# An attention and gated-MLP block on one core: moving the block transposes, scratch stores, weight loads and weight splits of the second norm

## The chip, the cores and the metric

The kernel runs on one core of one Trainium2 chip. The metric is the device time of one execution in microseconds (us); the time of a kernel is the median of several runs. The core has the engines PE (TensorE, matmuls), DVE (VectorE), ACT (ScalarE), POOL (GpSimd) and SP (SyncE). Each works through its own instructions in program order. Nearly all DMAs here are issued by SP on one queue.

## What is computed

Two residual branches on x of 2048 rows and 448 columns: attention with 16 heads of 28, then a gated MLP with a spatial mix over the rows. Each branch takes a layer norm that is scaled and shifted by columns computed from a vector c.

```python
h = layernorm(x) * (1 + ca) + sa
x = x + ga * attention(h, wqkv, wo)
h = layernorm(x) * (1 + cb) + sb              # the second norm
z = gelu(h @ w_in)                            # 2048 x 1792
z1, z2 = z[:, :896], layernorm(z[:, 896:])
g = w_sp @ z2 + b_sp                          # mixes rows
x = x + gb * ((z1 * g) @ w_out)
```

All data are float32.

## The kernel before, in words

Matmuls are made on float32 values split into a high and a low part, with products high-high, high-low and low-high; `STEPS` lists the eleven matmuls that make one product over the 448 rows of the contraction (three full chunks of 128, and a fourth of 64 whose high and low parts share one tile). Splitting a tile is a copy to the high part and a subtraction for the low one.

The order of instructions is written out by hand: each engine executes what the Python code issues, in that order, and waits on semaphores for its inputs. Tiles come from pools with a fixed number of buffers; seven PSUM banks go round (`bank`).

The stages are: the modulation columns and the first norm, the query, key and value products, attention (most of the span), the output product, the second norm, the first half of the w_in product (`z1_unit`), the second half (`z2_gemm`), the spatial mix, and the product with w_out. The change touches the stretch from the last output products to the end of the first half of the w_in product.

The 2048 rows form four groups of 512, index 0 to 3.

- `wo_tile(t)` (L1115) makes the output product of 128 rows on PE; `wo_add` (L1044) adds it to x on DVE and stores the result x2 to scratch through SP (L1047).
- `h2_stats(g)` (L1049) and `h2_norm(g)` (L1062) make the statistics and the normalized rows of group g; the power for the reciprocal deviation runs on POOL.
- Group 0 is transposed on PE by `ln_transpose` through `h2_first` (L1179). For its four column chunks, in the order 0, 2, 1, 3, ACT scales and copies, DVE subtracts, and then a function given as `after` is called with the chunk: here `late_tile` (L1210), which issues the last four output products in between.
- Groups 1 to 3 take another way. `h2_turn(g)` (L1079) transposes 32 x 32 blocks on DVE (L1086, four instructions). `h2_put(g)` (L1088) stores the blocks to a scratch tensor in DRAM with four DMAs (L1090). `h2_load(g)` (L1097) reads them back as rows of the transposed matrix with five DMAs (L1102 and L1104); it needs all four stores. `h2_group(g, cs)` (L1183) scales and splits the named column chunks, on ACT (L1187, L1188) and DVE (a subtraction, shown as L151).
- `z1_unit(g, f)` (L1196) makes eleven matmuls (L1199) for column block f of seven and row group g, the gelu on ACT (L1203) and the store of z1 (L1204). The loop at L1250 runs over 28 units.
- Between the units, `H2_AT` (L1240) says behind which unit which step of the norm is issued. `win_load` (L1108) loads rows of the other half of w_in; `win_prep` (L1112) splits them. For w_out, `wout_load` (L1224), `wout_part` (L1228: a product on DVE at L1230, a copy on ACT, a subtraction on DVE) and `wout_store` (L1236) run behind alternate units.

In a unit before the change, the w_out steps come ahead of the steps of `H2_AT`.

Of the kernel before, what the change touches and what calls it, by code (L numbers as in the profile page):

```python
# [99 lines left out]
def tile_adaln_mha_gmlp(ctx, tc, x, wqkv, wo, w_in, w_spT, b_sp, w_out, cT, w_mod0, w_mod, out):  # L100
# [881 lines left out]
    for h in range(H):  # L982
        a = h * NT
# [48 lines left out]
    t3 = ph3.enter_context(tc.tile_pool(name="t3", bufs=2))  # L1032
# [29 lines left out]
    def h2_norm(g):  # L1062
        mv, rs, _ = mv3.pop(g)
        if g == 0:
            nb = t3.tile([128, 4], F32, name="nb3")
            dve.scalar_tensor_tensor(out=nb, in0=mv[:, :, 0], scalar=-1.0, in1=rs, op0=ALU.mult, op1=ALU.mult)
        for tt in range(4):
            xt = x3[4 * g + tt]
            if g == 0:
                act.activation(xt[:, :D], xt[:, :D], AF.Identity, scale=rs[:, tt : tt + 1], bias=nb[:, tt : tt + 1])  # L1070
                pool.tensor_copy(xt[:, D:], xt[:, 384:D])
            else:
                dve.tensor_scalar(
                    out=xt[:, :D], in0=xt[:, :D], scalar1=mv[:, tt, 0:1], scalar2=rs[:, tt : tt + 1], op0=ALU.subtract, op1=ALU.mult
                )
# [3 lines left out]
    def h2_turn(g):  # L1079
        if g == 1:  # L1080
            b = fh.tile([128, 4 * 896], F32, name="turn", tag="heapE")
        else:
            b = t3.tile([128, 4, 512], F32, name="turn", tag="x3", bufs=3).rearrange("p a b -> p (a b)")
        blocks[g] = b[:, 0:1792].rearrange("p (b t i) -> p b t i", t=4, i=32)
        for tt in range(4):
            dve.transpose(blocks[g][:, :, tt, :], x3.pop(4 * g + tt)[:, :D])  # L1086

    def h2_put(g):  # L1088
        for a in range(4):
            sp.dma_start(  # L1090
                hs_scr[g - 1].rearrange("(b j) n -> j b n", j=32)[:, :, a * 128 : (a + 1) * 128],
                blocks[g][32 * a : 32 * a + 32].rearrange("p b t i -> p b (t i)"),
            )
# [14 lines left out]
    def win_load(i, p):  # L1108
        raw_in[i] = raw = p.tile([128, 896], F32, name="raw_in", bufs=1)
        sp.dma_start(raw, w_in[i * 128 : (i + 1) * 128, FH : 2 * FH])  # L1110

    def win_prep(i, lo_eng):  # L1112
        weight_part(w2, i, raw_in.pop(i), act, lo_eng)

    def wo_tile(t):  # L1115
        wo_mm(t, STEPS)
        wo_add(t)
# [59 lines left out]
    t3b = ph3.enter_context(tc.tile_pool(name="t3b", bufs=2))  # L1177

    def h2_first(after):  # L1179
        xns = [x3.pop(t) for t in range(4)]  # L1180
        ln_transpose(xns, t3b, h2T[0], cols["cb"], cols["sb"], (act,) * 4, (dve,) * 4, None, after)
# [14 lines left out]
    def z1_unit(g, f):  # L1196
        ps_t = bank("z1_ps")
        for j, (a, b) in enumerate(STEPS):
            pe.matmul(ps_t, w1[:, b, f * 128 : (f + 1) * 128], h2T[g][:, a, :], start=j == 0, stop=j == NST - 1)  # L1199
        if not zbuf:  # L1200
            zbuf.append(t3.tile([128, 4, 512], F32, name="z1t", tag="x3", bufs=3))
        zt = zbuf[0][:, (7 * g + f) % 4, :]
        act.activation(zt, ps_t, AF.Gelu_apprx_tanh)  # L1203
        sp.dma_start(z1_scr[f * 128 : (f + 1) * 128, g * 512 : (g + 1) * 512], zt)  # L1204
# [3 lines left out]
        h2_stats(1, (t - 8,))  # L1208

    def late_tile(c):  # L1210
        if c == 3:
            h2_turn(1)
        wo_tile({0: 12, 2: 13, 1: 14, 3: 15}[c])
        if c == 0:
            h2_norm(1)

    h2_first(late_tile)
    h2_put(1)
    win_load(0, t3)
    win_load(1, t3b)  # L1220
    wo3 = ph3.enter_context(tc.tile_pool(name="wo3", bufs=2))
    wouts = {}

# [15 lines left out]

    H2_AT = {}  # L1240
    for g, at_g in (
        (1, ((1, h2_load), (3, h2_group, (0, 2)), (4, h2_group, (1,)), (5, h2_group, (3,)))),
        (2, ((0, h2_stats), (1, h2_norm), (2, h2_turn), (3, h2_put), (5, h2_load))),
        (2, ((8, h2_group, (0,)), (9, h2_group, (2,)), (10, h2_group, (1,)), (11, h2_group, (3,)))),
        (3, ((4, h2_stats), (5, h2_norm), (6, h2_turn), (7, h2_put), (9, h2_load))),
        (3, ((13, h2_group, (0,)), (14, h2_group, (2,)), (15, h2_group, (1,)), (16, h2_group, (3,)))),
    ):
        for n, fn, *a in at_g:
            H2_AT.setdefault(n, []).append((fn, g, *a))
    for g in range(NG):  # L1250
        for f in range(7):
            z1_unit(g, f)
            for fn, n in ((wout_load, 10), (wout_part, 11), (wout_store, 12)):
                if 0 <= 7 * g + f - n < 14 and (7 * g + f - n) % 2 == 0:
                    fn((7 * g + f - n) // 2)
            for fn, *a in H2_AT.get(7 * g + f, ()):
                fn(*a)
            if g == 1 and f in (3, 5):
                win_prep(f // 4, dve)
                win_load(2 + f // 4, (t3, t3b)[f // 4])  # L1260
            if g == 2 and f in (3, 5):
                win_prep(2 + f // 4, dve)
# [417 lines left out]
```

## Time and profile before

| | us |
|---|---|
| Time, median of 3 runs | 1385.21 |
| Lowest and highest of these runs | 1382.43, 1385.46 |
| The profiled execution, its own time | 1383.42 |
| Span of the profile, from first to last instruction | 1381.6 |
| DVE busy | 1113.8 |
| ACT busy | 805.1 |
| POOL busy | 361.3 |

The profile is one execution on the chip. All positions in time are microseconds from the first instruction of the span. A line of the timeline gives the start, the length, the engine, the line of the kernel, the operation with output and input tiles, and how many instructions are merged; in brackets stands the idle time of the engine just ahead and what ended it. SPq is SP issuing DMAs, which isn't counted as busy. The granted clock is the share of full TensorE clock that the chip allowed in a stretch. A busy share is an average over stages with different limits; what a change in one stage is worth is read in that stage.

### The profile page before, as it was taken

The page shows a single profiled execution, that of the slowest core. Times are in us where ns is not written, and L with a number is a line of the kernel's source. Part 1 is how long each engine was busy: PE and PEld are TensorE (multiplying, and loading weights), DVE is VectorE, ACT ScalarE, POOL GpSimd, SP SyncE. Part 2 cuts the span into 40 slices and gives each one's busy share as a digit, 9 for nine tenths or more (in the row PEclk, how much of TensorE's full clock was granted, in tenths as well). Part 3 has the DMA queues.
Part 4 walks back from the last instruction along what each step waited for, and adds up shares of the span by engine and source line. Part 5 has one row for each costly group of instructions (what it writes and reads, how often), then busy time and mean ns, then how long its engine had stood idle before and what let it go on. Part 6 is the DMA issues. An engine that isn't in the chain of part 4 may idle for free.

```text
span 1381.6 us, 20787 instructions
## 1 busy us (share of the span) xinstructions
PE 1368.9 (99%) x7050; PEld 973.5 (70%) x7050; DVE 1113.8 (81%) x1764; ACT 805.1 (58%) x1475; POOL 361.3 (26%) x371
## 2 busy tenths in 40 slices
PE   9999999999999999999999999989999999999998
PEld 8888665555555565556565655877898888888898
DVE  7898899999999999999999971753367777999752
ACT  6623676767666776667676769435325544555411
POOL 2134335253535264745640011200021000000000
PEclk9999999999999999999999999999999999999999
DMA  8465756677677667876673010677604665787553
GB/s 284 135 172 182 231 162 210 198 222 234 208 213 211 215 201 225 237 240 209 216 230 97 23 44 22 207 229 219 233 16 142 224 197 195 245 285 262 186 163 108
DMA packets 144279, 260.21 MB, mean 188 GB/s; under 512 B 22120, under 2 KB 42986, under 8 KB 141626
## 3 DMA queue, kind: packets, MB, share of 16 engines
q1 hardware_dynamic: 141454, 254.69, 59.0%
q10 hardware_dynamic: 2718, 4.19, 0.8%
q8 instruction: 55, 0.90, 0.3%
q14 instruction: 52, 0.43, 0.1%
HBM read 177.67 MB, written 76.34 MB: 184 GB/s over the span
## 4 chain that ended last, share of the span: by engine, by line
PE 94%; DMA 2%; DVE 1%; issue 1%; SPq 1%; ACT 0%; POOL 0%; ACTq 0%; DVEq 0%; POOLq 0%
PE st_ps L744 18%; PE mt L712 17%; PE o_ps L759 16%; PE z_ps L1429 5%; PE acc L1497 5%; PE acc L1496 5%; PE acc L1498 5%; PE pq L407 5%; PE z_ps L1199 3%; PE wo_ps L831 2%; PE pv L389 2%; PE y_ps L1568 2%; PE y_ps L1569 2%; PE y_ps L1567 2%; PE acc L1504 1%
## 5 line engine op out<-in xcount | busy, mean ns | idle before, releaser
L717 DVE TENSOR_REDUCE pm<-mt 128x1 f32<-128x512 f32 x1024 | 627.8, 681 | 7.9 <-PE mt L712 7.7
L748 ACT ACTIVATE P<-st_ps 128x512 f32<-128x512 f32 x1024 | 512.6, 640 | 203.4 <-PE st_ps L744 200.9
L744 PE MATMUL st_ps<-qst,kst 128*128 128x512 f32 x1024 | 409.7, 410 | 0.0
L712 PE MATMUL mt<-kst,qst 128*128 128x512 f32 x1024 | 401.8, 392 | 0.0
L744 PEld LDWEIGHTS st_ps<-qst,kst 128*128 128x128 f32 x1024 | 191.3, 188 | 139.0 <-DVE pm L717 65.3
L759 PE MATMUL o_ps<-P,V 128*32 128x512 f32 x2048 | 240.0, 597 | 0.0
L712 PEld LDWEIGHTS mt<-kst,qst 128*128 128x128 f32 x1024 | 192.5, 188 | 34.7 <-ACT P L748 0.8
L869 POOL TENSOR_TENSOR ws_raw<-ws_raw 128x512 f32<-128x512 f32 x112 | 143.2, 1286 | 143.3 <-DMA ws_raw<-in_w_spT_dram 86.3
L1413 ACT ACTIVATE heapB<-raw_sp 128x512 fp32r<-128x512 f32 x156 | 96.7, 630 | 98.4 <-PE acc L1498 71.5
L759 PEld LDWEIGHTS o_ps<-P,V 128*32 128x32 f32 x2048 | 59.4, 109 | 126.8 <-issue 86.4
L1496 PE MATMUL acc<-heapB,heapA 128*128 128x512 f32 x312 | 121.4, 389 | 0.0
L1498 PE MATMUL acc<-heapB,heapA 128*128 128x512 f32 x312 | 121.4, 389 | 0.0
L765 DVE TENSOR_TENSOR osb<-osb,o_ps 128x512 f32<-128x512 f32 x82 | 56.4, 688 | 64.6 <-PE o_ps L759 63.1
L151 DVE TENSOR_TENSOR heapB<-raw_sp,heapB 128x512 fp32r<-128x512 f32 x112 | 74.6, 688 | 28.0 <-ACT heapB L1413 27.9
L1497 PE MATMUL acc<-heapB,heapA 128*128 128x512 f32 x222 | 86.5, 390 | 0.0
L1498 PEld LDWEIGHTS acc<-heapB,heapA 128*128 128x128 f32 x312 | 58.6, 188 | 12.2
L1496 PEld LDWEIGHTS acc<-heapB,heapA 128*128 128x128 f32 x312 | 58.6, 188 | 12.2
L407 PE MATMUL pq<-heapD,heapD 128*128 128x512 f32 x196 | 61.8, 390 | 0.0
L151 POOL TENSOR_TENSOR ws_raw<-ws_raw 128x512 fp32r<-128x512 f32 x44 | 56.7, 1288 | 3.5
L785 POOL TENSOR_TENSOR osb<-osb,rb 128x512 f32<-128x512 f32 x15 | 19.3, 1289 | 112.1 <-DVE pm L717 80.9
L1497 PEld LDWEIGHTS acc<-heapB,heapA 128*128 128x128 f32 x222 | 41.7, 188 | 8.8 <-DVE heapB L151 0.3
L171 POOL TENSOR_TENSOR rsz<-rsz,mhalf 128x1 f32<-128x1 f32 x16 | 14.2, 890 | 116.0 <-DVE rsz L170 116.0
(224 smaller groups left out, 1674.2 us busy)
## 6 DMA issues: line engine op xcount, KB each, us to landing
ws_raw<-in_w_spT_dram SPq DMA_DIRECT2D x136, 256.0 KB
ws_scr<-ws_raw SPq DMA_DIRECT2D x112, 256.0 KB
ws_raw<-ws_scr SPq DMA_DIRECT2D x88, 256.0 KB
raw_sp<-ws_scr SPq DMA_DIRECT2D x88, 256.0 KB
raw_sp<-in_w_spT_dram SPq DMA_DIRECT2D x68, 256.0 KB
wl_scr<-ws_raw SPq DMA_DIRECT2D x44, 256.0 KB
kst<-qk_scr SPq DMA_DIRECT2D x45, 224.0 KB
qst<-qk_scr SPq DMA_DIRECT2D x45, 224.0 KB
```

Of the source, the lines that this page charges most:

```text
L151: eng.tensor_tensor(out=dst, in0=a, in1=hi.bitcast(F32), op=ALU.subtract)
L407: pe.matmul(pq, wqk[:, b, m * 128 : (m + 1) * 128], hT[g][:, a, :], start=j == 0, stop=j == NST - 1)
L712: pe.matmul(mt, qst[h % 3][:, t * 128 : (t + 1) * 128], kst[h % 3][:, kb * 512 : (kb + 1) * 512], start=True, stop=True)
L717: dve.tensor_reduce(out=pms[h][:, t, kb : kb + 1], in_=mt, axis=AX.X, op=ALU.max)
L744: pe.matmul(st, kst[h % 3][:, kt * 128 : (kt + 1) * 128], qst[h % 3][:, qb * 512 : (qb + 1) * 512], start=True, stop=True)
L748: act.activation(p, st, AF.Exp, scale=SCALE)
L759: pe.matmul(o[32 * qb : 32 * qb + 32, :], V[:, u % NT, h, :], ptiles.pop((u, qb)), start=u == a, stop=u == e - 1)
L869: pool.tensor_tensor(out=a, in0=a, in1=b, op=ALU.add if W_SUMS[v][2] > 0 else ALU.subtract)
L1413: act.activation(hi, raw[0], AF.Copy)
L1496: pe.matmul(o, zh[:, c], hi, start=p < 2 and kt == 0, stop=False, skip_group_check=p > 1)
L1497: pe.matmul(o, zh[:, c], lo, start=False, stop=False, skip_group_check=p > 1)
L1498: pe.matmul(o, zl[:, c], hi, start=False, stop=kt == 3, skip_group_check=p > 1)
```

## The change

`late_tile` issues the four block transposes of group 1 and their four stores behind the output product of chunk 2, where before the transposes stood ahead of the output product of chunk 3 and the stores behind the whole of `h2_first`. The first two loads of w_in rows move from ahead of the loop to behind units 4 and 5. The loads of group 1's transposed rows move from behind unit 1 to behind unit 0. In every unit the steps of `H2_AT` now come ahead of the w_out steps, and the w_out splits and stores come one unit later than before (offsets 12 and 13 in place of 11 and 12).

```diff
     def late_tile(c):
-        if c == 3:
-            h2_turn(1)
         wo_tile({0: 12, 2: 13, 1: 14, 3: 15}[c])
         if c == 0:
             h2_norm(1)
+        elif c == 2:
+            h2_turn(1)
+            h2_put(1)
 
     h2_first(late_tile)
-    h2_put(1)
-    win_load(0, t3)
-    win_load(1, t3b)
...
     for g, at_g in (
-        (1, ((1, h2_load), (3, h2_group, (0, 2)), (4, h2_group, (1,)), (5, h2_group, (3,)))),
+        (1, ((0, h2_load), (3, h2_group, (0, 2)), (4, h2_group, (1,)), (5, h2_group, (3,)))),
...
     for g in range(NG):
         for f in range(7):
             z1_unit(g, f)
-            for fn, n in ((wout_load, 10), (wout_part, 11), (wout_store, 12)):
+            for fn, *a in H2_AT.get(7 * g + f, ()):
+                fn(*a)
+            if (g, f) in ((0, 4), (0, 5)):
+                win_load(f - 4, (t3, t3b)[f - 4])
+            for fn, n in ((wout_load, 10), (wout_part, 12), (wout_store, 13)):
                 if 0 <= 7 * g + f - n < 14 and (7 * g + f - n) % 2 == 0:
                     fn((7 * g + f - n) // 2)
-            for fn, *a in H2_AT.get(7 * g + f, ()):
-                fn(*a)
```

## The prediction, made before the changed kernel was run

> **What bounds the kernel now.** I read the page first, then the timeline of TensorE (PE) around the second norm.
>
> ```profile
> span 1381.6 us, 20787 instructions
> PE 1368.9 (99%) x7050; PEld 973.5 (70%) x7050; DVE 1113.8 (81%) x1764; ACT 805.1 (58%) x1475; POOL 361.3 (26%) x371
> ```
>
> PE is busy for 99% of the span, so the end moves only where PE waits or runs slowly. Nearly all of its waiting lies in the first-half GEMM loop (L1199): 28 units of 11 matmuls, seven units for each row group of 512. The timeline gives start, length, work, and in brackets the idle time ahead.
>
> ```profile
> 900.54 17.86 PE L1199 MATMUL z_ps<-heapB,heapA 128*128 128x512 f32 x78
> 919.00 1.42 PE L1199 MATMUL z_ps<-heapB,heapA 128*128 128x512 f32 x5 [0.60 <-ACT heapB L1188]
> 920.85 1.23 PE L1199 MATMUL z_ps<-heapB,heapA 128*128 128x512 f32 x3 [0.43 <-ACT heapB L1188]
> 924.89 18.46 PE L1199 MATMUL z_ps<-heapB,heapA 128*128 128x512 f32 x68 [2.82 <-DVE heapB L151]
> 943.19 2.20 PE L1199 MATMUL z_ps<-heap,heapA 128*128 128x512 f32 x9
> 948.21 34.59 PE L1199 MATMUL z_ps<-heap,heapA 128*128 128x512 f32 x145 [2.82 <-DVE heap L151]
> 982.64 0.77 PE L1429 MATMUL z_ps<-heapD,heapB 128*128 128x448 f32 x3
> ```
>
> The first burst is row group 0 and one matmul of the next (the text calls the four groups index 0 to 3, the fourth column chunk of a group chunk 3): 17.86/78 = 0.229 us a matmul, 2.52 a unit. At that pace 308 matmuls take 70.5 us; the loop takes 982.64 - 900.54 = 82.1. So **11.6 us** are lost. The idle entries are 0.60 + 0.43 + 2.82 at the start of index 1 and 2.82 in index 2: 6.67. Most of the rest is the clock. In these windows of L1199 the columns are stretch, length, PE busy, weight loads busy, granted clock, DMA share and GB/s.
>
> ```profile
> 900.50:918.40 17.90, 17.86 (x78) 14.48 (x78) 1.00 0.80 238
> 924.90:943.20 18.30, 18.30 (x69) 14.85 (x70) 0.84 0.78 233
> 948.20:982.60 34.40, 34.39 (x145) 28.20 (x145) 0.96 0.68 224
> ```
>
> A mean clock of 0.84 over 18.3 us costs 2.9, and 0.96 over 34.4 costs 1.4: 4.3 us in which PE ran at half speed just behind the idle stretches. 6.7 + 4.3 leaves 0.6 for refilling after four stops.
>
> **The first stall (index 1)** comes through ACT and DVE:
>
> ```profile
> 904.59 0.60 ACT L1203 ACTIVATE z1t<-z_ps 128x512 f32<-128x512 f32 x1
> 910.73 0.60 ACT L1203 ACTIVATE z1t<-z_ps 128x512 f32<-128x512 f32 x1 [1.90 <-PE z_ps L1199]
> 916.10 0.82 ACT L1187 ACTIVATE hfull<-heapB,col_sb,col_cb 128x512 f32<-128x512 f32 x1 [4.77 <-DMA heapB<-hs_scr]
> ```
>
> ```profile
> 920.83 0.69 DVE L151 TENSOR_TENSOR heapB<-hfull,heapB 128x512 fp32r<-128x512 f32 x1 [1.16 <-ACT heapB L1188]
> 921.44 2.20 DVE L1055 BATCH_NORM_STATS2 st<-xl 128x6 f32<-128x448 f32 x4
> 924.15 0.69 DVE L151 TENSOR_TENSOR heapB<-hfull,heapB 64x512 fp32r<-64x512 f32 x1
> ```
>
> ACT waits 4.77 us for the scratch load of the transposed rows, scales and splits the four column chunks from 916.10, and the last split part (chunk 3, behind the statistics of index 3) ends at 924.84: T + 8.74, if T is the first scaling. PE goes on at 924.89. The load was late because of SP, which issues every DMA here in order:
>
> ```profile
> 894.70 8.26 SPq L1047 DMA_DIRECT2D x_scr<-xl  x4
> 903.01 3.14 SPq L1090 DMA_DIRECT2D hs_scr<-turn  x4
> 906.20 2.12 SPq L1110 DMA_DIRECT2D raw_in<-in_w_in_dram  x2
> 909.44 2.35 SPq L1102 DMA_DIRECT2D heapB<-hs_scr  x3
> ```
>
> The stores of the blocks go out behind the last of four x2 stores; two w_in loads follow; the loads go out 6.43 us after the first block store, and the first one lands 6.66 later (909.44 to 916.10).
>
> **The second stall (index 2)** has another cause:
>
> ```profile
> 944.83 0.62 DVE L1230 TENSOR_TENSOR raw_out<-raw_out,bc_gb 128x448 f32<-128x448 f32 x1 [5.00 <-DMA raw_out<-in_w_out_dram]
> 947.47 0.69 DVE L151 TENSOR_TENSOR heap<-hfull,heap 64x512 fp32r<-64x512 f32 x1 [0.74 <-ACT heap L1188]
> ```
>
> In unit 11 DVE stands 5.00 us before the w_out rows of L1230, with the split of chunk 3 (and ACT's copies) queued behind. PE starts 0.05 us after that split ends.
>
> **The change part by part.** Instructions are neither added nor removed; positions move.
>
> *Transposes earlier.* DVE around them:
>
> ```profile
> 896.28 0.69 DVE L151 TENSOR_TENSOR heapB<-hfull,heapB 128x512 fp32r<-128x512 f32 x1
> ...
> 897.42 0.69 DVE L151 TENSOR_TENSOR heapB<-hfull,heapB 128x512 fp32r<-128x512 f32 x1
> 898.51 0.62 DVE L1046 TENSOR_TENSOR xl<-xl,wo_ps 128x448 f32<-128x448 f32 x1 [0.41 <-PE wo_ps L831]
> ...
> 899.88 2.22 DVE L1086 STREAM_TRANSPOSE turn<-x 128x448 f32<-128x448 f32 x4
> ```
>
> The four transposes (2.22) now start at 897.42, in the place of the split of chunk 1, and end at 899.65. Behind them come the split of chunk 1 (to 900.3), the addition of wo tile 14 (900.9), the split of chunk 3 (901.5) and the addition of tile 15 (902.1). PE begins the loop at 900.54 and reads chunk 1's low part at its ninth step (902.4) and chunk 3 at its tenth (902.6): 2.1 and 1.1 us of cover. Cost nothing; if DVE ran over 1.1 us later, each further microsecond is one of PE.
>
> *Stores directly behind, w_in later, load one unit earlier.* SP issues the block stores at 899.7 instead of 903.0, 3.3 earlier, into an idle queue (next to last number: DMA share; last: GB/s):
>
> ```profile
> 896.00:898.00 2.00, 2.00 (x12) 1.85 (x11) 2.00 (x4) 0.90 (x2) 0.00 (x0) 1.00 0.07 26
> 904.00:906.00 2.00, 2.00 (x11) 1.65 (x9) 1.17 (x7) 1.43 (x3) 0.65 (x1) 1.00 0.78 199
> 908.00:910.00 2.00, 2.00 (x10) 1.65 (x10) 2.00 (x5) 0.60 (x1) 0.00 (x0) 1.00 0.98 206
> 914.00:916.00 2.00, 2.00 (x11) 1.65 (x10) 0.00 (x0) 0.00 (x0) 0.00 (x0) 1.00 1.06 366
> ```
>
> With the 6.43 us of before they have landed at 906.1. By then SP has issued the x2 stores 14 and 15 (to 903.7) and the z1 store of unit 0, whose gelu ends at 905.19. So the loads go out at 906.1 instead of 909.44. Landing: at most 6.66 later as before, 912.8. But the queue ahead held two w_in loads (0.92 MB) and two z1 stores; now two x2 stores (0.46 MB) and one z1 store (0.26 MB fewer). 0.72 MB less at the 366 GB/s of the full queue is 2.0 us: **910.8**, which I take. ACT can't start chunk 0 before the gelu of unit 3 ends (911.33), so T = 911.3 and the last split ends at 920.1. PE wants it at the tenth step of unit 7: 900.54 + 7 x 2.52 + 9 x 0.229 = 920.2. The stall goes, with 0.1 to spare; T = 912.8 would leave 1.4. Below that, no gain is to be had: PE doesn't start the loop earlier.
>
> What 1.4 us of idle do to the clock no row shows: 0.60 and 0.43 left it at 1.00, 2.82 halved it, which cost 2.9 and 1.4. So 0 to 2.9 beside the 1.4, and 0 is nearer to the rows of under 1 us.
>
> ```profile
> 924.00:925.00 1.00, 0.11 (x1) 0.11 (x1) 0.81 (x2) 0.00 (x0) 0.73 (x1) 0.50 0.73 260
> ```
>
> The Trainium skill ("TensorE: Matmul & The Clock Gate", Part 1, "What's actually happening") says that the clock falls to half after at least one idle window of about 3.4 us and comes back after a busy one. By it neither 2.82 us here should have halved the clock, and 1.4 us would cost 1.4 alone; the trace shows 0.50 behind 2.82, so the row decides and I keep the upper end.
>
> *The same order for index 2 and 3: what is late next.* The block stores of index 2 follow the z1 store of unit 3 and go out at about 911.8:
>
> ```profile
> 915.28 3.43 SPq L1090 DMA_DIRECT2D hs_scr<-turn  x4
> ...
> 922.80 1.27 SPq L1102 DMA_DIRECT2D heap<-hs_scr  x3
> ```
>
> Store to load took 7.52 us; that gives loads at 919.3, landed at 926.0. The moved w_in loads lie in this stretch, one ahead of the loads and one behind. ACT takes the four chunks behind the gelus of units 8 to 11; the last gelu is ready at 900.54 + 12 x 2.52 = 930.8, so chunk 3 is split by 933.5. PE wants it at 937.9: 4.4 us to spare.
>
> *w_out splits one unit later, behind the steps of the norm.* The split of chunk 3 no longer waits for w_out; the second stall goes (2.82 + 1.4 + its refill). The wait itself remains: in unit 12, DVE's product waits for the w_out rows and ACT's copy for DVE; behind them stand the w_in split of unit 12, then gelu 13 and the chunks of index 3. The rows of index 3, and the first w_out load:
>
> ```profile
> 928.04 2.21 DVE L1086 STREAM_TRANSPOSE turn<-xl 128x448 f32<-128x448 f32 x4
> ```
>
> ```profile
> 940.45 0.38 SPq L1226 DMA_DIRECT2D raw_out<-in_w_out_dram  x1
> ```
>
> The transposes of index 3 ended 5.4 us behind the last split of index 1 (930.25 - 924.84), so now at 925.5; with the 7.52 of index 2 the loads go out at 933.0 and, 3 us of issuing later, the first w_out load at 936.0. From issue to use it took 4.4 (940.45 to 944.83): DVE goes on at 940.4, ACT behind its copy at 941.0. ACT then has one w_in copy (0.9), four gelus (0.60 each), four chunks (0.82 + 0.6 each) and one more w_out copy (0.6): 9.6 us, to 950.6, and DVE's split ends 0.7 later at 951.3. PE wants chunk 3 of index 3 at 955.5. Seven PSUM banks let PE run on meanwhile. Hidden, with 4.2 to spare.
>
> **Sum.** 11.6 lost, all of it removed, less 0.2 for the thin margin at index 1: 11.4. The profiled execution took 1383.42 (span 1381.6): 1372.0. The four times shown, 1382.43, 1383.42, 1385.21 and 1385.46, have a mean of 1384.1, 0.7 above it, so I predict **1372.7**.
>
> **Rivals.** *A, the forecast, 0.66:* 1371 to 1374.
> *B, the first stall shrinks but stays, 0.17:* the loads land as slowly as before, because the block stores and loads are limited by themselves. For it: 199 GB/s with 0.78 to 0.98 of the engines' time. Against: 0.72 MB less ahead. 1.4 to 4.3 us remain: 1374 to 1377.
> *C, for index 1 the change doesn't do what it says, 0.08:* the blocks leave earlier but a wait on SP (a store, or a load that waits for all four block stores) eats the 3.3 us. Then only the second stall goes, 2.82 + 1.4 + 0.2: about 1379.7. Against: SP has nothing to wait for between 903.7 and 905.2.
> *E, the w_out wait on ACT becomes the bound, 0.09:* as worked out, ACT may be freed up to 941.0 + 4.2 = 945.2 without harm; later than that, every microsecond is one of PE, plus up to 2.9 of slow clock. It ends slower than before if w_out lands past 945.2 + 11.4 - 2.9 = 953.7, 17.7 us after its issue at 936.0; a few microseconds earlier it is no difference. For it: SP, one queue, holds all. Against: 4.4 us in the trace. Slower 0.05, same 0.04.
>
> **How the numbers follow.** Range 1370.0 (the lowest run less 11.6, and 0.8 of scatter) to 1378.0 (B's end and a microsecond): A and B, 0.83. Faster by over 0.2% (2.8 us, about what a measurement of this kernel can tell from no change): A, B and C, 0.91; same 0.04; slower 0.05.
>
> **What would show it.** L1199 in one burst of 308 matmuls in 70 to 71 us at clock 1.00; L1090 issued first near 899.7 and L1102 near 906; ACT's L1187 of index 1 starting straight behind the gelu of unit 3; DVE's wait at L1230 still there, in unit 12, with PE busy beside it. An idle entry of over 1 us near 918 to 922 speaks for B; ACT behind L1230 with PE idle past 945 for E. I am wrong if the loads land after 912, or if the next stage gives back what this one gains.

## The result, and the profile after

| | before | after |
|---|---|---|
| median, us | 1384.19 (4 runs, 1382.43 to 1385.46) | 1370.17 (4 runs, 1369.99 to 1370.81) |
| profiled execution, us | 1383.42 | 1370.01 |
| span, us | 1381.6 | 1368.2 |

The changed kernel takes 0.990 of the time before, with a 95% interval of 0.9883 to 0.9918. The forecast was 1372.7 us, in a range of 1370.0 to 1378.0; the measured time is 2.5 us below the one and 0.2 us above the lower end of the other.

The busy line of the changed kernel's page:

```profile
PE 1361.4 (100%) x7050; PEld 968.0 (71%) x7050; DVE 1112.8 (81%) x1764; ACT 805.2 (59%) x1475; POOL 361.8 (26%) x371
```

The same instructions ran; PE's busy time fell by 7.5 us, 5.5 of it in the loop L1199, since a matmul at half clock counts as busy for longer (up to 0.79 us each in that loop before, at most 0.47 now). The timeline of PE through the loop L1199:

```profile
899.28 35.19 PE L1199 MATMUL z_ps<-heapB,heapA 128*128 128x512 f32 x154
934.31 35.07 PE L1199 MATMUL z_ps<-heap,heapA 128*128 128x512 f32 x154
969.22 0.77 PE L1429 MATMUL z_ps<-heapD,heapB 128*128 128x448 f32 x3
```

and its window (stretch, length, PE busy, weight loads busy, granted clock, DMA share, GB/s):

```profile
899.30:969.20 69.90, 69.90 (x308) 57.55 (x307) 1.00 0.87 274
```

No bracket with an idle time is left, and the clock is 1.00 throughout. The loop takes 969.22 - 899.28 = 69.9 us in place of 82.1. Its DMA share rose from 0.73 over the whole loop of before (227 GB/s) to 0.87 (274): nearly the same bytes, 18.6 and 19.2 MB, in less time.

The first row group that comes through scratch memory (index 1), on SP, ACT and DVE of the changed kernel:

```profile
898.41 3.01 SPq L1090 DMA_DIRECT2D hs_scr<-turn  x4
901.52 2.69 SPq L1047 DMA_DIRECT2D x_scr<-xl  x2
904.30 0.38 SPq L1204 DMA_DIRECT2D z_scr<-z1t  x1
905.31 1.27 SPq L1102 DMA_DIRECT2D heapB<-hs_scr  x3
```

```profile
909.47 0.60 ACT L1203 ACTIVATE z1t<-z_ps 128x512 f32<-128x512 f32 x1 [1.90 <-PE z_ps L1199]
909.97 0.80 ACT L1187 ACTIVATE hfull<-heapB,col_sb,col_cb 128x512 f32<-128x512 f32 x1
...
940.99 0.58 ACT L1230 ACTIVATE wout<-raw_out 128x448 fp32r<-128x448 f32 x1 [7.94 <-DVE raw_out L1228]
...
947.41 0.58 ACT L1230 ACTIVATE wout<-raw_out 128x448 fp32r<-128x448 f32 x1 [1.29 <-DVE raw_out L1228]
```

```profile
918.01 0.69 DVE L151 TENSOR_TENSOR heapB<-hfull,heapB 64x512 fp32r<-64x512 f32 x1
...
940.33 0.62 DVE L1228 TENSOR_TENSOR raw_out<-raw_out,bc_gb 128x448 f32<-128x448 f32 x1 [7.04 <-DMA raw_out<-in_w_out_dram]
...
951.72 0.69 DVE L151 TENSOR_TENSOR heap<-hfull,heap 64x512 fp32r<-64x512 f32 x1 [1.16 <-ACT heap L1188]
```

The loop began 1.26 us earlier than in the profile of before, so 1.26 us of every position here come from that. ACT goes straight from the gelu of unit 3 to the first scaling; the last split of index 1, behind DVE's statistics of index 3, ends at 918.70, and PE wants it at 899.28 + 7 x 2.497 + 9 x 0.227 = 918.80 (seven units of eleven matmuls at the pace of the burst, 0.227 us, and nine matmuls more). DVE still waits 7.04 us for w_out and ACT 7.94, now in unit 12 and with PE busy beside it, since PE's burst from 934.31 on has no idle entry.

### The profile page after: what moved, and what is told of

Same layout as the page of the kernel before. It is cut to its first block, busy times and chain, and to the rows that moved or that the text cites. A ratio compares the mean times of both kernels' runs of the same rounds, so it can differ in the third digit from the quotient of the medians.

```text
span 1368.2 us, 20793 instructions
## 1 busy us (share of the span) xinstructions
PE 1361.4 (100%) x7050; PEld 968.0 (71%) x7050; DVE 1112.8 (81%) x1764; ACT 805.2 (59%) x1475; POOL 361.8 (26%) x371
## 4 chain that ended last, share of the span: by engine, by line
PE 96%; issue 1%; DVE 1%; DMA 1%; POOL 0%; ACTq 0%; DVEq 0%; POOLq 0%; SPq 0%
PE st_ps L744 18%; PE mt L712 17%; PE o_ps L759 16%; PE z_ps L1429 5%; PE acc L1498 5%; PE acc L1497 5%; PE acc L1496 5%; PE z_ps L1199 5%; PE pq L407 5%; PE wo_ps L831 3%; PE pv L389 2%; PE y_ps L1569 2%; PE y_ps L1567 2%; PE y_ps L1568 2%; PE acc L1506 1%
## 5 line engine op out<-in xcount | busy, mean ns | idle before, releaser
L1432 ACT ACTIVATE z<-z_ps 128x448 f32<-128x448 f32 x32 | 17.4, 545 | 48.0 <-PE z_ps L1429 48.0
```

## The experiments

Theory: two stalls were removed. The first (index 1) was a matter of when the loads of the transposed rows land, the second (index 2) of chunk 3 standing behind the w_out wait on DVE and ACT; each also cost a stretch of half clock. The rivals were that the two are separate and simply add up, that w_out was hidden anyway, and that the w_out wait becomes the new bound. The diffs are against the changed kernel where nothing else is said. Each comparison has the kernel before on the same chip, 1383.5 to 1383.7 us.

**e1: the kernel before, a second profile.**

> The kernel before, once more, for a second profile of it. Theory: 1.26 us of the measured gain lie ahead of the loop, where the two kernels are the same, and come from a clock of 0.74 to 0.92 between 5 and 15 us that this execution of before happened to have; the loop L1199 takes 82.1 us again, give or take one half-clock window of about 1.5 us, so 1382 to 1386, and the slow clock at the start need not appear. Rival: before always starts with the slow clock, and the change removes it: 0.74 to 0.92 at 5 to 15 us again.

Measured: 1383.62 us, ratio 1.0002 [0.9993, 1.0011]. Two rows of the timeline of its loop, and the early windows of the first profile of before, with the granted clock as the third number from the end:

```profile
924.06 17.32 PE L1199 MATMUL z_ps<-heapB,heapA 128*128 128x512 f32 x68 [2.82 <-DVE heapB L151]
...
947.91 35.29 PE L1199 MATMUL z_ps<-heap,heapA 128*128 128x512 f32 x145 [4.50 <-DVE heap L151]
```

```profile
5.00:10.00 5.00, 4.88 (x37) 4.76 (x36) 4.05 (x12) 1.60 (x5) 1.61 (x2) 0.92 1.04 401
10.00:15.00 5.00, 4.68 (x25) 4.23 (x24) 3.75 (x12) 3.27 (x8) 0.00 (x0) 0.74 1.03 402
```

In e1 these two early windows are at 1.00. Of the thirteen profiles of this study three have the slow start (before, e4 and e6), two of them of kernels with the early stores; it belongs to an execution, not to a kernel. So the 1.26 us ahead of the loop, most of which that start accounts for, are no effect of the change. The loop of e1 took 983.04 - 899.47 = 83.6 us, 1.5 longer than in the first profile. PE ran only one half-clock window (3.41 us) behind the first stall, came to index 2 two microseconds sooner, and waited there 4.50 in place of 2.82: its restart, 947.91 against 948.21, was set by w_out, whose first rows DVE used at 944.53 against 944.83, and not by PE.

**e2: the part for index 1 alone.**

```diff
+            for fn, n in ((wout_load, 10), (wout_part, 11), (wout_store, 12)):
+                if 0 <= 7 * g + f - n < 14 and (7 * g + f - n) % 2 == 0:
+                    fn((7 * g + f - n) // 2)
             for fn, *a in H2_AT.get(7 * g + f, ()):
                 fn(*a)
             if (g, f) in ((0, 4), (0, 5)):
                 win_load(f - 4, (t3, t3b)[f - 4])
-            for fn, n in ((wout_load, 10), (wout_part, 12), (wout_store, 13)):
-                if 0 <= 7 * g + f - n < 14 and (7 * g + f - n) % 2 == 0:
-                    fn((7 * g + f - n) // 2)
```

> The changed kernel, with the w_out steps back in their old places (split in unit 11, ahead of the steps of the norm). Theory: the first stall is gone, so PE reaches row group index 2 some 9 us earlier, while the w_out rows land at about 940 as in the changed kernel; chunk 3 of index 2 is then split at 943.6 and PE wants it at 936.4: the second stall grows from 2.8 to about 7.3 us, and with 1.4 to 2.9 us of half clock behind it the time is 1378.9 to 1380.5. Rival (the two stalls are separate and keep their prices): the second stall is 2.8 us again and costs 4.5 with its clock: 1374 to 1376.

Measured: 1378.94 us, ratio 0.9971 [0.996, 0.9981]. Its PE and DVE:

```profile
943.19 34.68 PE L1199 MATMUL z_ps<-heap,heapA 128*128 128x512 f32 x145 [6.69 <-DVE heap L151]
```

```profile
939.81 0.62 DVE L1228 TENSOR_TENSOR raw_out<-raw_out,bc_gb 128x448 f32<-128x448 f32 x1 [7.71 <-DMA raw_out<-in_w_out_dram]
941.08 0.62 DVE L151 TENSOR_TENSOR wout<-raw_out,wout 128x448 fp32r<-128x448 f32 x1 [0.64 <-ACT wout L1230]
942.44 0.69 DVE L151 TENSOR_TENSOR heap<-hfull,heap 64x512 fp32r<-64x512 f32 x1 [0.74 <-ACT heap L1188]
```

The first stall is gone, and a good part of what that frees is given back: the second stall grows from 2.82 to 6.69 us. In index 2 PE is ready for its tenth step 8.9 us earlier than in the first profile of before (936.50 against 945.39), while DVE's first use of w_out moves by only 5.0 us (939.81 against 944.83).

**e3: the w_out part alone** (against the kernel before).

```diff
-            for fn, n in ((wout_load, 10), (wout_part, 11), (wout_store, 12)):
+            for fn, *a in H2_AT.get(7 * g + f, ()):
+                fn(*a)
+            for fn, n in ((wout_load, 10), (wout_part, 12), (wout_store, 13)):
                 if 0 <= 7 * g + f - n < 14 and (7 * g + f - n) % 2 == 0:
                     fn((7 * g + f - n) // 2)
-            for fn, *a in H2_AT.get(7 * g + f, ()):
-                fn(*a)
```

> The kernel before, with only the w_out splits and stores one unit later and behind the steps of the norm. Theory: the first stall stays (0.6, 0.4 and 2.8 us of idle, about 2.9 us of half clock), the second goes: 1377.5 to 1380. Rival (w_out is hidden anyway and the second stall only follows from the first, through late chunks of index 2): the second stall stays, 1383 to 1385.

Measured: 1377.66 us, ratio 0.9957 [0.9945, 0.997].

```profile
923.61 17.30 PE L1199 MATMUL z_ps<-heapB,heapA 128*128 128x512 f32 x68 [2.81 <-DVE heapB L151]
940.75 35.07 PE L1199 MATMUL z_ps<-heap,heapA 128*128 128x512 f32 x154
```

The first stall stays, index 2 and 3 run through. The two parts alone gain 4.7 (e2) and 6.0 (e3), the whole change 13.5 against the same runs of before (14.0 against its own): about 3 us more than their sum. Beside the first stall the second cost 6.0 us; with the first gone it costs 8.8 (13.5 less 4.7), because PE then arrives at it earlier by more than w_out does.

**e4: w_in loads ahead of the loop.**

```diff
     h2_first(late_tile)
+    win_load(0, t3)
+    win_load(1, t3b)
...
-            if (g, f) in ((0, 4), (0, 5)):
-                win_load(f - 4, (t3, t3b)[f - 4])
```

> The changed kernel, with the first two loads of w_in back ahead of the loop. Theory: SP spends 2.1 us on them ahead of the loads of the transposed rows, and 0.92 MB stand ahead in the queue; the first scaling of index 1 moves from 910.0 to 911.5 to 912.6, chunk 3 is late by the same 1.5 to 2.6 us, and half clock may add 0 to 2.9: 1371.5 to 1375.7. Rival (the early stores alone leave room enough): 1370.2, within 0.5.

Measured: 1374.88 us, ratio 0.9937 [0.9925, 0.995]. PE, SP and ACT:

```profile
922.47 17.35 PE L1199 MATMUL z_ps<-heapB,heapA 128*128 128x512 f32 x68 [2.36 <-DVE heapB L151]
```

```profile
906.74 1.89 SPq L1102 DMA_DIRECT2D heapB<-hs_scr  x3
```

```profile
913.66 0.81 ACT L1187 ACTIVATE hfull<-heapB,col_sb,col_cb 128x512 f32<-128x512 f32 x1 [2.44 <-DMA heapB<-hs_scr]
```

**e5: transposes and stores late.**

```diff
     def late_tile(c):
+        if c == 3:
+            h2_turn(1)
         wo_tile({0: 12, 2: 13, 1: 14, 3: 15}[c])
         if c == 0:
             h2_norm(1)
-        elif c == 2:
-            h2_turn(1)
-            h2_put(1)
 
     h2_first(late_tile)
+    h2_put(1)
```

> The changed kernel, with the block transposes and their stores back in their old places (w_in still later, loads still behind unit 0). Theory: SP issues the stores at about 901.9 in place of 898.4, the loads go out at 908.8 in place of 905.3, the first scaling of index 1 moves from 910.0 to 912.2 to 913.5: PE idles 2.2 to 3.5 us at the tenth step of unit 7 and runs one or two windows at half clock (1.7 or 2.9): 1374 to 1376.6. Rival (with the w_in loads out of the way the late stores are covered): 1370.2, within 0.5.

Measured: 1371.91 us, ratio 0.9914 [0.9899, 0.9929], less than expected.

```profile
920.14 15.71 PE L1199 MATMUL z_ps<-heapB,heapA 128*128 128x512 f32 x68 [1.45 <-DVE heapB L151]
```

```profile
908.60 1.29 SPq L1102 DMA_DIRECT2D heapB<-hs_scr  x3
```

```profile
911.34 0.82 ACT L1187 ACTIVATE hfull<-heapB,col_sb,col_cb 128x512 f32<-128x512 f32 x1 [1.53 <-DMA heapB<-hs_scr]
```

The two together separate the two edits for index 1. From the issue of the first load to its use take 913.66 - 906.74 = 6.92 us in e4, with the two w_in loads ahead of it, and 911.34 - 908.60 = 2.74 in e5, without. The two runs differ in other transfers too; the changed kernel differs from e4 by w_in alone. There the semaphore of this load was complete at 908.17, 2.86 us behind its issue at 905.31; in e4 it was at 913.58, 6.84 behind. So the 0.92 MB of w_in cost 4.0 us in the queue and, with e4's loop beginning 1.16 us later, 0.3 us on SP. They are the larger cause (e4 lost 4.7 us against the changed kernel, e5 1.7). The late stores cost 1.45 us of idle, and the clock stayed at 1.00 behind it (68 matmuls in 15.71 us, 0.231 each, against 0.255 in e4).

**e6: the loads of index 1 behind unit 1.**

```diff
-        (1, ((0, h2_load), (3, h2_group, (0, 2)), (4, h2_group, (1,)), (5, h2_group, (3,)))),
+        (1, ((1, h2_load), (3, h2_group, (0, 2)), (4, h2_group, (1,)), (5, h2_group, (3,)))),
```

> The changed kernel, with the loads of the transposed rows of index 1 back behind unit 1. Theory: the z1 store of unit 1 is ready at 905.1, and SP couldn't send the loads before 905.3 anyway, since the block stores had not landed: no difference, 1370.2 within 0.5. Rival (the unit's place on SP matters): the loads go out a unit, 2.5 us, later, and 2 to 4 us are lost: 1372 to 1375.

Measured: 1370.92 us, ratio 0.9905 [0.989, 0.9919]. The first half of the loop is one burst again:

```profile
900.60 35.19 PE L1199 MATMUL z_ps<-heapB,heapA 128*128 128x512 f32 x154
```

The time is 0.75 us above the changed kernel's, a little more than was expected, but the loop has no idle time, and this execution has the slow clock at 5 to 15 us, so its loop starts at 900.60. The first load was complete 10.36 us behind the start of the loop in place of 8.89 (910.96 and 908.17), and ACT began the first scaling at 10.68 and 10.69. So this edit of the change gains 1.5 us of spare time, and no time that the profiles show.

**e7 and e8: which half of the w_out edit matters.** e7 keeps the steps of the norm ahead and takes the w_out offsets back to 11 and 12; e8 keeps 12 and 13 and puts the w_out steps ahead again.

```diff
-            for fn, n in ((wout_load, 10), (wout_part, 12), (wout_store, 13)):
+            for fn, n in ((wout_load, 10), (wout_part, 11), (wout_store, 12)):
```

> The changed kernel, with the w_out splits and stores one unit earlier again (11 and 12), still behind the steps of the norm. Theory: being behind the split of chunk 3 is what takes the second stall away, the unit is not needed for it; but ACT then also has the gelu of unit 12 and a third w_out copy ahead of chunk 3 of index 3, which had 1.4 us to spare: 1370.2 to 1371.5. Rival (the later unit is what matters): the second stall is back, 1375 to 1380.

> The changed kernel, with the w_out steps ahead of the steps of the norm again, but still one unit later (12 and 13). Theory: unit 12 has no step of the norm, so chunk 3 of index 2 isn't held up and the second stall stays away by this alone; in unit 16 chunk 3 of index 3 comes behind a w_out split, 1.4 us later, which just uses up its spare time: 1370.2 to 1371. Rival (the order in the unit is what matters): a stall of 2 us or more in index 3, with half clock: 1373 to 1376.

Measured: e7 1372.17 us, ratio 0.9914 [0.9899, 0.9929]; e8 1371.6 us, ratio 0.9908 [0.9891, 0.9924]. One row of PE each, e7 first:

```profile
955.51 15.73 PE L1199 MATMUL z_ps<-heap,heapA 128*128 128x512 f32 x68 [1.08 <-DVE heap L151]
```

```profile
955.29 15.75 PE L1199 MATMUL z_ps<-heap,heapA 128*128 128x512 f32 x68 [1.30 <-DVE heap L151]
```

Both are slower than was expected (1371.5 and 1371 at most). Either half alone removes the second stall. With either alone a stall of a microsecond appears in index 3, at the tenth step again: chunk 3 there then stands behind a third w_out split, whose product on DVE waits for its rows until 951.65 (e7) and 951.90 (e8). Both halves together keep it just clear.

**e9: a measured idle time of 1.9 us.** Four statistics more on DVE ahead of the last split of index 1; their results go nowhere.

```diff
+    def hold(g, n):
+        for _ in range(n):
+            st = t3.tile([128, 6], F32, name="st3", bufs=4)
+            dve.bn_stats(out=st, in_=x3[12][:, :D])
...
-        (1, ((0, h2_load), (3, h2_group, (0, 2)), (4, h2_group, (1,)), (5, h2_group, (3,)))),
+        (1, ((0, h2_load), (3, h2_group, (0, 2)), (4, h2_group, (1,)), (5, hold, 4), (5, h2_group, (3,)))),
```

> The changed kernel, with four more statistics of rows that DVE has already used, 2.1 us, ahead of the last split of index 1 (their results go nowhere). It measures what an idle time of 1.9 us does to the clock: idle times of 1.08 to 1.45 us left it at 1.00 in the experiments so far, 2.36 and more halved it for one or two windows of 3.3 us. Theory: there is a bound between 1.45 and 2.36, and 1.9 lies on either side of it: 1372.1 without half clock, 1373.8 with one window. Rival (a full window of 3.4 us without work is needed, the drop behind 2.36 had another cause): 1372.1 and a clock of 1.00.

Measured: 1372.63 us, ratio 0.9923 [0.9909, 0.9938]; single runs 1374.11, 1372.16, 1373.04 and 1372.22. The profile is of the slowest, PE's row and three windows (granted clock third from the end):

```profile
921.25 17.32 PE L1199 MATMUL z_ps<-heapB,heapA 128*128 128x512 f32 x68 [1.91 <-DVE heapB L151]
```

```profile
921.00:922.00 1.00, 0.75 (x3) 0.67 (x4) 0.97 (x3) 0.00 (x0) 0.00 (x0) 0.96 0.86 293
922.00:923.00 1.00, 1.00 (x4) 0.70 (x4) 1.00 (x4) 0.60 (x1) 0.00 (x0) 0.50 1.02 315
...
926.00:927.00 1.00, 1.00 (x6) 0.82 (x5) 0.00 (x0) 0.88 (x2) 0.00 (x0) 1.00 0.99 352
```

1.91 us of idle halved the clock in this execution. Two of the others are 1.9 us faster, about what one half-clock window of 3.41 us costs (1.7), and agree with the figure without it. Only the slowest has a profile, but each execution has its mean clock: 1.000 in these two, 0.999 in the other two.

**e10: w_out loads just ahead of their splits.**

```diff
-            for fn, n in ((wout_load, 10), (wout_part, 12), (wout_store, 13)):
+            for fn, n in ((wout_load, 12), (wout_part, 12), (wout_store, 13)):
```

> The changed kernel, with the w_out loads two units later, just ahead of their splits. Theory (rival E of the prediction, with the spare time as measured, 1.4 us in place of 4.2): ACT and DVE wait for w_out up to about 942 and again in unit 14; chunk 3 of index 3 is split near 956.3, PE wants it at 953.8: 1.5 to 4 us of idle, and half clock: 1372 to 1376. If the spare time were 4.2 as predicted: 1370.2.

Measured: 1384.25 us, ratio 1.0005 [0.9995, 1.0014]: far slower than expected, the whole gain is gone. Its PE (the waits alone) and ACT (the w_out copies):

```profile
956.02 1.52 PE L1199 MATMUL z_ps<-heap,heapA 128*128 128x512 f32 x3 [2.76 <-ACT heap L1188]
958.59 17.96 PE L1199 MATMUL z_ps<-heap,heapA 128*128 128x512 f32 x68 [1.05 <-DVE heap L151]
981.73 0.88 PE L1429 MATMUL z_ps<-heapD,heapB 128*128 128x448 f32 x3 [2.96 <-ACT z1t L1203]
989.03 0.88 PE L1429 MATMUL z_ps<-heapD,heapB 128*128 128x448 f32 x3 [2.59 <-ACT z1t L1203]
```

```profile
960.38 0.58 ACT L1230 ACTIVATE wout<-raw_out 128x448 fp32r<-128x448 f32 x1 [2.57 <-DVE raw_out L1228]
...
967.06 0.58 ACT L1230 ACTIVATE wout<-raw_out 128x448 fp32r<-128x448 f32 x1 [4.29 <-DVE raw_out L1228]
...
973.92 0.58 ACT L1230 ACTIVATE wout<-raw_out 128x448 fp32r<-128x448 f32 x1 [4.47 <-issue]
```

One round of the wait between two of these copies, on ACT, SP and DVE:

```profile
962.18 0.59 ACT L1203 ACTIVATE z1t<-z_ps 128x512 f32<-128x512 f32 x1
```

```profile
962.85 0.40 SPq L1204 DMA_DIRECT2D z_scr<-z1t  x1
963.30 0.45 SPq L1224 DMA_DIRECT2D raw_out<-in_w_out_dram  x1
```

```profile
966.40 0.62 DVE L1228 TENSOR_TENSOR raw_out<-raw_out,bc_gb 128x448 f32<-128x448 f32 x1 [2.99 <-DMA raw_out<-in_w_out_dram]
```

The first w_out rows were used only 1.2 us later than in the changed kernel (941.50 against 940.33). What costs is that the wait comes back at every second unit: a w_out load stands on SP behind a z1 store, that behind a gelu, the gelu behind the w_out copy on ACT, and the copy behind the load before (gelu to 962.77, z1 store 962.85, load 963.30, product 966.40, copy 967.06). The copies follow each other at 6.7 to 6.9 us (960.38, 967.06, 973.92), two units of PE take 5.0. ACT falls further behind until PE waits for the gelus that free its PSUM banks, in the next stage too.

**e11: w_out loads earlier.**

```diff
             z1_unit(g, f)
+            if 0 <= 7 * g + f - 9 < 14 and (7 * g + f - 9) % 2 == 0:
+                wout_load((7 * g + f - 9) // 2)
             for fn, *a in H2_AT.get(7 * g + f, ()):
...
-            for fn, n in ((wout_load, 10), (wout_part, 12), (wout_store, 13)):
+            for fn, n in ((wout_part, 12), (wout_store, 13)):
```

> The changed kernel, with the w_out loads one unit earlier and ahead of the loads of the transposed rows, so that the wait for the first of them all but goes. Theory: that wait (7.9 us on ACT) lies wholly beside PE: no difference, 1370.2 within 0.5, and chunk 3 of index 3 is split several us earlier. Rival (it costs PE something that the trace doesn't name): 1 us or more faster.

Measured: 1370.16 us, ratio 0.9904 [0.9889, 0.9918].

```profile
934.09 0.58 ACT L1230 ACTIVATE wout<-raw_out 128x448 fp32r<-128x448 f32 x1 [1.14 <-DVE raw_out L1228]
```

```profile
945.84 0.69 DVE L151 TENSOR_TENSOR heap<-hfull,heap 64x512 fp32r<-64x512 f32 x1 [1.16 <-ACT heap L1188]
```

ACT's wait falls from 7.94 to 1.14 us and chunk 3 of index 3 is split 5.9 us earlier, for no gain: the wait was hidden. None of the runs beats the changed kernel by more than its scatter.

## Why the prediction was right, and where its sizes were off

- **Two stalls and the half clock behind them, 11.6 us: right, 0.6 too small.** The measured pace is 0.227 us a matmul, where the prediction divided a burst's length by its count, the tail of the last matmul included. At 0.227 the loop lost 12.2 in the first profile. From the 11.4 of the forecast to the 14.0 measured, that is 0.6, and the 0.2 left for a thin margin that wasn't needed; then 1.26 lies ahead of the loop, mostly the slow start of the profiled execution of before, and 0.6 is the difference between the profiled executions and the medians. Against the larger set of runs of before (1383.62) the gain is 13.5, and e1, without the slow start, lost 13.6 in its loop: the first profile had a cheap pair of stalls. The measured time lies outside rival A's 1371 to 1374, and it took some luck to lie in the range, whose lower end was set by the lowest run and the scatter. B and C are ruled out: no idle entry is left, and the loads went out as forecast.
- **Block stores at 899.7, loads at 906.1: right.** 898.41 and 905.31, or 899.67 and 906.57 with the 1.26 us added back.
- **Landing at 910.8, of which 2.0 us less queue: the term was mis-sized.** It took the queue's bytes at 366 GB/s and put the landing 4.7 us behind the issue. The first load was complete after 2.86 us, at 908.17, so less queue was worth 3.8; against e4 the 0.92 MB of w_in alone were worth 4.0. This does not reach the time, because ACT is held by the gelu of unit 3 (to 909.97) either way, as the prediction said. From that scaling to the end of the last split took 8.73 us (8.74 in the forecast), and the margin was 0.1 us, as predicted.
- **Transposes ahead of two splits at no cost: right.** Loop and first unit run without a gap.
- **What 1.4 us of idle do to the clock, 0 to 2.9, taken as 0: right.** The profiled executions of e5 (1.45), e7 and e8 stayed at 1.00; the change itself didn't test it, for no idle time was left. The Trainium skill's page "TensorE: Matmul & The Clock Gate" (Part 1, "What's actually happening") asks for an idle window of about 3.4 us; here 1.91 already halved the clock in one execution, so the measurement decides. Its remark there that the window runs freely fits the grid of 3.41 us in these traces (last section).
- **The second stall goes: right,** and e3 shows it without the first part. That the two are linked the prediction didn't say: it summed them, and e2 shows that the first part alone gives back a good part of its gain.
- **Spare time in index 2, 4.4 us: 1.4 too much, hidden.** The last split ends at 933.29 and PE wants it at 936.28, 3.0 later. The gelu of unit 10 had waited 1.41 us for an earlier store of z1.
- **Spare time in index 3, 4.2 us: wrong by 2.9, though hidden.** It was 953.76 - 952.41 = 1.35. Counted from the start of the loop, ACT had the first w_out copy behind it 1.8 us later than forecast (42.3 in place of 40.5; the rows were used 5.7 us behind their issue in place of 4.4, and the 0.6 of DVE's product ahead of the copy had been left out); the work behind it took 0.5 longer, for the next w_out copy waits 1.29 us for DVE; and PE was 0.5 faster.
- **Rival E: the mechanism right, its price wrong.** The prediction let w_out land up to 17.7 us after its issue before the kernel would be slower than before. In e10 the first rows were used 1.2 us later than in the changed kernel, and the gain was gone. The step took the wait as one event; it is a cycle through SP, DMA, DVE and ACT that comes round seven times.

## What to carry to other kernels

A stall that ends at a transfer isn't worth what it shows: remove one upstream and PE arrives earlier at the next, by more than the transfer does (8.9 against 5.0 us in e2), so price each with the other gone, and take both out together. Where queues run in order, look for cycles (a load behind a store behind a result behind the load before): if one round takes longer than the work that it feeds, slack of a few microseconds is gone in a few rounds. What stands ahead in a DMA queue, weights that nobody needs yet above all, can delay a small urgent load by more than its bytes suggest: 4.0 us here, where 0.92 MB at the 366 GB/s of the full queue would be 2.5.

## What was not expected of the hardware

The clock halved behind idle times of 1.91, 2.36, 2.76, 2.82, 4.50 and 6.69 us, stayed at 1.00 behind 1.08, 1.30 and 1.45, and also behind the 2.96 and 2.59 of e10. So the length of one idle time doesn't decide it. In every trace's record of the clock the stretches at half clock in the loop last 3.41 or 6.83 us, and the full ones between two of them are multiples of 3.41: the clock changes on a grid. These are steps of that grid in e10 (PE's busy time is the second figure, the clock the third from the end):

```profile
953.13:956.54 3.41, 0.65 (x3) 0.30 (x2) 1.55 (x3) 2.97 (x6) 0.00 (x0) 1.00 0.32 121
977.02:980.43 3.41, 1.75 (x9) 1.28 (x7) 0.53 (x1) 0.00 (x0) 0.00 (x0) 1.00 0.69 225
980.43:983.85 3.42, 2.12 (x10) 1.99 (x11) 0.72 (x2) 1.55 (x3) 0.00 (x0) 1.00 0.39 146
987.26:990.67 3.41, 1.64 (x8) 1.53 (x9) 1.45 (x4) 3.24 (x7) 0.00 (x0) 1.00 0.41 147
```

PE was idle for 2.76 us of the first, and the step behind it ran at 0.50. The 2.96 us ahead of 981.73 are cut in two, 1.67 and 1.29, and the 2.59 ahead of 989.03 leave at most 1.77 in one step: the clock stayed at 1.00. In the loops of all thirteen profiles, and in the stage behind it in e10, a step with 1.91 us or more of idle time was followed by half clock, one with 1.77 or less, begun at full clock, was not, and full clock came back behind the first step at half clock with no more than 0.39 idle. (In the last microseconds of e10 a step with 1.91 idle left the clock at 1.00, so the bound lies near that.) So where a stall falls on the grid would decide how many windows follow, and on which side 1.9 us falls; no run moved the one against the other on purpose. It may also be why the kernel before scattered by 3 us and the changed one, without idle time in the loop, by 0.8; that was not tested by itself.

The slow start in three of thirteen profiles belongs to neither kernel: their loops begin at 900.44 to 900.60 us, those of the others at 899.02 to 899.77. Its cause stays open.
